# A new opening table, row-wise exponentials for two batches, and block products for one more unit in an attention-and-MLP kernel

## The chip, the cores and the metric

The kernel runs on one core of one Trainium2 chip. The time is device microseconds of that core, median of three runs. The core has five engines that the text names as the profile does: PE (matrix products) with PEld (its weight loads), DVE (vector work), ACT (activations and copies), POOL (vector work without access to the accumulators) and SP, which only issues DMA transfers. Each engine carries out its own list of instructions in order, and waits where an instruction needs another engine's result or a landed transfer.

## The reference

```python
a = softmax(phi, axis=tokens)                 # phi: 8 batches, 8 heads, 576 tokens, 32 memory rows
k_m = einsum('bhsm,bhsd->bhmd', a, k)         # 32 memory rows of 64 per head
v_m = einsum('bhsm,bhsd->bhmd', a, v)
scores = (q @ k_m.T) / sqrt(64)
attn = softmax(scores, axis=memory rows)
x = (attn @ v_m), heads side by side          # 4608 tokens x 512
h = x @ w_in                                  # 512 x 2048, given as 64-bit floats
g = h - tanh(h)
out = g @ w_out                               # 2048 x 512, given as 64-bit floats
```

All 4608 tokens (8 batches of 576) go through both halves. The result is 32-bit.

## The kernel before

**Tiling.** The 4608 tokens are 18 units of 256 (`u` = 0 to 17); the hidden width 2048 is four blocks of 512 (`fb` = 0 to 3). A unit and a block make one slot: `mm1` (L540) computes h for the slot, ACT and DVE turn it into g by a polynomial in three steps (`g1` L555 with its squares L547 and L560 on ACT, `g2` L564, then the 16-bit high part L569 and the low part L574), and `mm2` (L617) or `mm2_blocks` (L666, L673) multiplies g with w_out. Numbers are carried as pairs of 16-bit high and low parts, so that a product of two pairs is three 16-bit products.

**Attention.** For each batch the memory rows of phi, k and v are pooled (`V`, L194 and L202, accumulated in `pkv`), normed (`N`, L207 to L210), turned (`U`, L231), and multiplied with q (`S`, L246); softmax over the memory rows follows (`AM`, `AE`, `AD`, `AT`), and the result is split into high and low (`AS`, L481 and L483). The values are not multiplied with the attention weights but with w_in first: `P` (L492) makes a 256-row matrix per batch and block, high part on ACT (L505), low part on DVE (`PL`, L510) or by PE and ACT (`PLp`, L517 and L519). `mm1` then takes attention weights times that matrix.

**The softmax of phi.** `X` (L144) takes the largest phi of each memory row on DVE and spreads it on a diagonal matrix (L146); a product with ones (`XP`, L155) puts the maxima on every partition; DVE subtracts them (`Y`, L160 and L166) from a second copy of phi that was loaded with the tokens on the partitions (`FA`, L104); ACT takes the exponentials (L180).

**The weights.** `T` converts a pair of weight blocks from 64-bit floats with six integer operations on DVE (L354, L359, L364), and ACT makes the high halves (L376). Low halves come in one of three ways: `Lp` on PE and ACT (four products, L397 and L398, and one copy, L400), `L` on ACT and POOL (L405, L408), `Lv` on DVE (L389). There are 16 such pairs.

**The order.** Up to the second block of unit 4 the order is a table of words, `START`, read from left to right; a word that stands twice or three times is done in as many parts. The words `i0:us`, `o2:gg` and the like issue the load of a weight block into a buffer of that name. `Z` issues products into a result that nobody reads (`warm`, L742). All engines' lists follow from this one table. After it a loop over slots 18 to 71 issues `mm1`, `g1`, `g2`, a slot of `mm2` two slots behind, and tasks from tables by slot: the remaining batches' attention, the block forms of w_out (`G`, L599), and in `PLAN_C` the sums over the weights that test whether all numbers are in the range for which the fast path is exact. That test ends in one number, `bad`; where it is set, a slow path is run.

**Block products.** Units 5 to 17 use `mm2_blocks`: the high-times-high product is done whole (eight products of 512 columns, L666), and the two mixed ones by seven products of half-size blocks (28 products of 256 columns, L673), for which DVE makes four sums of blocks of g per slot (`a_forms`, L587) and eight of w_out once (`b_form`, L599). Units 0 to 4 use `mm2`, 24 products of 512 columns. At a unit's end `evict` (L722 to L734) puts the parts together and stores them.

## Time and profile before

| | before |
|---|---|
| median of three runs | 678.07 us (677.39 to 678.25) |
| the profiled execution | 677.7 us |
| its span (first to last instruction) | 675.9 us |
| PE busy | 640.8 us, 95% |
| DVE busy | 510.7 us, 76% |
| ACT busy | 375.7 us, 56% |
| POOL busy | 256.1 us, 38% |
| mean granted PE clock | 0.993 |

The span leaves 1.8 us of the profiled execution outside it. Busy times are sums over the span without overlaps; a PE product is counted from its start to a modelled end, so PE looks busier than its work. In the views quoted below, a row of the timeline reads: start, duration, engine, line, operation, output and inputs, shapes, count, and in brackets the idle time before it and what ended it. A window reads: its bounds, its length, then the busy time of PE, PEld, DVE, ACT and POOL with the number of instructions, the granted PE clock, the busy share of the DMA engines and GB/s. A row of a group reads: count, busy time and mean nanoseconds of one, idle time before them.

### The profile page before, as it was taken

To read this page: it belongs to the slowest core of one execution; us is meant where nothing else is said; L and a number is where in the kernel's file an instruction comes from. 1 tells how busy PE (TensorE), PEld (TensorE's weight loads), DVE (VectorE), ACT (ScalarE), POOL (GpSimd) and SP (SyncE) were. 2 spreads that over 40 slices of the span, in tenths; PEclk is the share of its full clock that TensorE was granted. 3 is DMA by queue.
4 is the path that set the end of the run, shared out by engine and by line. 5 is a ranking of instruction groups with operands and counts; after the bars stand their busy time and mean duration, and the time that the engine had idled before them with its cause. 6 is when DMAs were issued, how large, how long until landed. Compare 5 with 4: busy or idle time off the path is not lost.

```text
span 675.9 us, 15441 instructions
## 1 busy us (share of the span) xinstructions
PE 640.8 (95%) x6628; PEld 447.2 (66%) x6628; DVE 510.7 (76%) x784; ACT 375.7 (56%) x506; POOL 256.1 (38%) x170
## 2 busy tenths in 40 slices
PE   4678989999999999999999999999999999999996
PEld 1336465565646567786767777777777777887874
DVE  4688999989655577965697868886888586867673
ACT  1558477765533355653565455646554587666541
POOL 0032623423111334452345344534453555455521
PEclk9979999999999999999999999999999999999999
DMA  9679663422313132214331523152415224234201
GB/s 342 265 280 363 244 180 125 172 99 86 119 63 107 60 125 72 66 62 176 102 106 42 192 80 121 49 192 68 134 49 190 72 103 121 72 118 137 77 32 37
DMA packets 26428, 86.16 MB, mean 127 GB/s; under 512 B 2928, under 2 KB 3184, under 8 KB 25584
## 3 DMA queue, kind: packets, MB, share of 16 engines
q1 hardware_dynamic: 25056, 82.87, 35.9%
q10 hardware_dynamic: 1296, 2.23, 0.9%
q8 instruction: 54, 0.88, 0.6%
q14 instruction: 22, 0.18, 0.1%
HBM read 73.55 MB, written 11.53 MB: 126 GB/s over the span
## 4 chain that ended last, share of the span: by engine, by line
PE 69%; DVE 6%; ACT 1%; DMA 1%; issue 0%; SPq 0%; DVEq 0%; ACTq 0%
PE hs L540 19%; PE o L666 12%; PE x L673 12%; PE o L673 9%; PE o L617 7%; PE h L540 2%; PE pp L492 2%; PE pkv L194 2%; DVE f L587 2%; PE o1h L617 2%; DVE h L555 1%; DVE h L564 1%; PE psc L246 1%; DMA kv<-in_kva_dram 1%; ACT u L547 1%
## 5 line engine op out<-in xcount | busy, mean ns | idle before, releaser
L574 POOL TENSOR_TENSOR g<-h,g 128x1024 f16<-128x1024 f32 x64 | 145.2, 2268 | 321.8 <-ACT g L569 212.5
L540 PEld LDWEIGHTS <-ph 128*128 128x128 f16 x2304 | 176.6, 98 | 21.9 <-issue 6.5
L540 PE MATMUL hs<-ah,ph 128*128 128x256 f16 (+3 forms) x1088 | 145.8, 248 | 0.0
L555 DVE SCALAR_TENSOR_TENSOR h<-hs,u 128x1024 f32<-128x1024 f32 x52 | 63.5, 1221 | 96.3 <-ACT u L547 96.3
L569 ACT ACTIVATE g<-h 128x1024 f16<-128x1024 f32 x72 | 76.0, 1055 | 94.8 <-DVE h L564 86.0
L540 PE MATMUL hs<-al,ph 128*128 128x256 f16 (+3 forms) x544 | 122.2, 248 | 0.0
L560 ACT ACTIVATE u<-u,beta 128x1024 f32<-128x1024 f32 x72 | 82.6, 1148 | 61.5 <-DVE h L555 61.0
L666 PE MATMUL o<-wout_hi,g 128*128 128x512 f16 x416 | 100.7, 380 | 1.5 <-DVE r L733 1.5
L564 DVE SCALAR_TENSOR_TENSOR h<-u,h 128x1024 f32<-128x1024 f32 x72 | 89.0, 1236 | 5.0 <-ACT u L560 4.6
L673 PEld LDWEIGHTS <-f 128*128 128x128 f16 x832 | 81.3, 98 | 9.5
L617 PEld LDWEIGHTS <-g 128*128 128x128 f16 x480 | 45.7, 98 | 59.4 <-issue 4.1
L547 ACT ACTIVATE u<-hs 128x1024 f32<-128x1024 f32 x52 | 53.0, 1019 | 53.1 <-PE hs L540 53.1
L617 PE MATMUL o<-wout_hi,g 128*128 128x512 f16 x256 | 78.6, 380 | 1.3 <-DVE g L574 0.8
L673 PE MATMUL x<-bt,f 128*128 128x256 f16 x624 | 76.6, 273 | 0.0
L673 PEld LDWEIGHTS <-g 128*128 128x128 f16 x624 | 60.5, 98 | 21.7 <-issue 0.8
L666 PEld LDWEIGHTS <-g 128*128 128x128 f16 x416 | 38.4, 98 | 48.5 <-issue 13.6
L587 DVE TENSOR_TENSOR f<-g 128x512 f16<-128x512 f16 x104 | 59.7, 614 | 3.9 <-POOL g L574 3.4
L540 PE MATMUL h<-ah,ph 128*128 128x256 f16 (+2 forms) x448 | 55.8, 243 | 0.0
L540 PE MATMUL h<-al,ph 128*128 128x256 f16 (+2 forms) x224 | 48.0, 242 | 1.0 <-DVE al L483 1.0
L617 PE MATMUL o<-wout_lo,g 128*128 128x512 f16 x128 | 48.6, 380 | 0.0
L510 DVE SCALAR_TENSOR_TENSOR ph<-pp,ph 128x1024 f16<-128x1024 f32 x30 | 36.5, 1216 | 1.9 <-ACT ph L505 1.7
L505 ACT ACTIVATE ph<-pp 128x1024 f16<-128x1024 f32 x32 | 32.5, 1016 | 4.0 <-PE pp L492 4.0
(134 smaller groups left out, 945.6 us busy)
## 6 DMA issues: line engine op xcount, KB each, us to landing
kv<-in_kva_dram SPq DMA_DIRECT2D x20, 516.0 KB, 4.0
q<-in_qt_dram SPq DMA_DIRECT2D x16, 576.0 KB, 4.1
chk<-in_w_in_dram SPq DMA_DIRECT2D x16, 512.0 KB, 5.2
chk<-in_w_out_dram SPq DMA_DIRECT2D x16, 512.0 KB, 3.4
out_dram<-r SPq DMA_DIRECT2D x25, 256.0 KB, 2.6
kv<-in_kva_dram SPq DMA_DIRECT2D x6, 1032.0 KB, 10.6
raws<-in_w_in_dram SPq DMA_DIRECT2D x12, 512.0 KB, 6.0
raw<-in_w_out_dram SPq DMA_DIRECT2D x12, 512.0 KB, 6.7
```

The source lines that it names most:

```text
L510: nc.vector.scalar_tensor_tensor(pl, pa, S_P / (S_V * S_W), ph, op0=ALU.mult, op1=ALU.subtract)
L540: nc.tensor.matmul(hp[:, k, tu : tu + w], px[:, g, cs], d[ax][:, g, ta : ta + w], start=(n == 0), stop=(n == 5),)
L547: nc.scalar.activation(uu, hp, AF.Square, scale=1.0 / (S_A * S_P))
L555: nc.vector.scalar_tensor_tensor(h3, hp, C2 * S_G / (S_A * S_P), uu, op0=ALU.mult, op1=ALU.mult)
L560: nc.scalar.activation(uu, uu, AF.Square, bias=c["beta"])
L564: nc.vector.scalar_tensor_tensor(h3, uu, CC, h3, op0=ALU.add, op1=ALU.mult)
L569: nc.scalar.activation(gg[:, 0], h3, AF.Copy)
L574: eng.tensor_tensor(gg[:, 1], h3, gg[:, 0], op=ALU.subtract)
L587: nc.vector.tensor_tensor(o, x, y, op=op)
L617: nc.tensor.matmul(o, gx[:, k, P * tt : P * tt + P], wx[:, 4 * fb + k, :], start=(first and k == 0 and wx is wout_hi and gx is gh), stop=( ...
L666: nc.tensor.matmul(o[th], gg[:, 0, k, P * th : P * th + P], wout_hi[:, 4 * fb + k, :], start=(first and k == 0), stop=False)
L673: nc.tensor.matmul(dst, a(1 - n, kk), b(n, kk), start=(new and kk == 0 and n == 0), stop=(end and kk == 1 and n == 1))
```

## The change

1. **Constants first.** The 16-bit identity and its scaled copies (L1052 to L1054) are made by DVE ahead of all else, so `Z` products may begin at once; in the kernel before, DVE converted the first weight pair ahead of them. A `Z` word is now two products, not four, and there are 26 of them, not 4.
2. **Exponentials in rows.** For batches 0 and 1, `X` takes the negated maxima (L144's operation, no diagonal); `YX` takes the exponentials on ACT straight from the row-wise copy of phi with the maxima as bias, two instructions of 576 columns; `XT` turns them with ten products by the identity on PE, and ACT copies the result out of the accumulators in two pieces. The second copy of phi (`FA0`, `FA1`), the diagonal, the product with ones and the subtraction are gone for these two.
3. **The table.** `START` is a new order throughout. Counted by words: low halves by PE for three pairs, not five; by DVE for four more blocks (two pairs); one `PLp` became `PL`; one low part of g moved from POOL to DVE, one multiplication and one split from DVE to POOL. The block forms `G` of w_out stand in its last third, and the forms of the first block of unit 4 at its end.
4. **Unit 4 by block products.** `mm2_blocks` and `evict` now serve unit 4 too, with the sums of its blocks of g by DVE.
5. **Norms.** For three of the four blocks of w_in, DVE adds the four squared rows together (`SS`, two additions), so that `NI` takes 4 products, not 16.
6. **The end.** In the last unit the second half's products are split by column halves, the first into an accumulator of their own, so that half of its result is put together earlier; the half is stored by one transfer, issued by ACT, not by two. The number `bad` is read before the last `evict`.

On DVE, the first instructions of the program. `wt` are converted weights, `raw` their 64-bit source, `nid`, `nidp`, `idw` the identities, `pt` phi in rows. Before:

```order
L354 TENSOR_SCALAR wt_105<-raw_101 128x512
L354 TENSOR_SCALAR wt_106<-raw_103 128x512
L359 SCALAR_TENSOR_TENSOR wt_105<-raw_101,wt_105 128x512
L359 SCALAR_TENSOR_TENSOR wt_106<-raw_103,wt_106 128x512
L364 SCALAR_TENSOR_TENSOR wt_105<-raw_101,wt_105 128x512
L364 SCALAR_TENSOR_TENSOR wt_106<-raw_103,wt_106 128x512
L1052 TENSOR_SCALAR nid_66<-ident 128x128
L1053 TENSOR_SCALAR nidp<-ident 128x128
L1054 TENSOR_SCALAR idw<-ident 128x128
L354 TENSOR_SCALAR wt_137<-raws_134 128x512
```

Now:

```order
L1093 TENSOR_SCALAR nid_66<-ident 128x128
L1094 TENSOR_SCALAR nidp<-ident 128x128
L1095 TENSOR_SCALAR idw<-ident 128x128
L380 TENSOR_SCALAR wt_108<-raw_101 128x512
L380 TENSOR_SCALAR wt_109<-raw_106 128x512
L385 SCALAR_TENSOR_TENSOR wt_108<-raw_101,wt_108 128x512
L385 SCALAR_TENSOR_TENSOR wt_109<-raw_106,wt_109 128x512
L390 SCALAR_TENSOR_TENSOR wt_108<-raw_101,wt_108 128x512
L390 SCALAR_TENSOR_TENSOR wt_109<-raw_106,wt_109 128x512
L186 TENSOR_REDUCE mx_124<-pt_122 128x2
L380 TENSOR_SCALAR wt_141<-raws_126 128x512
```

The identities went ahead of the first conversion, and the maxima of phi (L186, before L144), which stood behind four conversions, now stand behind one.

On PE, what stands ahead of the first pooling `pkv`. `pw` are low halves of weights (five pairs of them in the whole table before, three now), `pmx` the spread maxima, `pet` and `pel` the turned exponentials. Before, with twelve `warm` products ahead of the first `pw` and four behind it:

```order
L397 MATMUL pw_212<-wt_182,idw 128x512
L398 LDWEIGHTS nid_66
L398 MATMUL pw_212<-win_hi,nid_66 128x512
L397 MATMUL pw_212<-wt_183,idw 128x512
L398 LDWEIGHTS nid_66
L398 MATMUL pw_212<-win_hi,nid_66 128x512
L155 MATMUL pmx_228<-dg_208,ones 128x256
L194 MATMUL pkv_234<-kv_164,e_158 32x129 x16
L194 MATMUL pkv_234<-kv_168,e_158 32x129 x16
L202 MATMUL pkv_234<-kt_166,e_158 32x129 x8
```

Now, with 36 `warm` products ahead of the first `pw`:

```order
L423 MATMUL pw_206<-wt_142,idw 128x512
L424 LDWEIGHTS nid_66
L424 MATMUL pw_206<-win_hi,nid_66 128x512
L200 MATMUL pet_211<-ident,pt_122 128x128 x8
L202 MATMUL pel_212<-ident,pt_122 64x128 x2
L786 LDWEIGHTS nid_66
L786 MATMUL warm<-nid_66 128x512
...
L220 MATMUL pkv_234<-kv_166,e_229 32x129 x16
```

`pw_212` was the fourth pair in this place and `pw_206` is the second: two pairs' low halves left PE's list ahead of the pooling, the product with ones left it, and the ten turning products came in.

On DVE, the end of the program. `r` are the results, `x`, `o` and `oh` accumulators, `bad` the number read. Before:

```order
L722 SCALAR_TENSOR_TENSOR r_8605<-x,r_8605 128x256
L723 SCALAR_TENSOR_TENSOR r_8606<-x,r_8605 128x256
L724 TENSOR_TENSOR r_8605<-r_8605,r_8606 128x256
L725 TENSOR_TENSOR r_8606<-r_8606 128x256
L733 SCALAR_TENSOR_TENSOR r_8605<-o_8449,r_8605 128x512
L730 SCALAR_TENSOR_TENSOR r_8606<-o_8450,r_8606 128x256 x2
L1061 TENSOR_LOAD bad
```

Now:

```order
L925 TENSOR_LOAD bad
L765 SCALAR_TENSOR_TENSOR r_8676<-x,r_8676 128x256
L766 SCALAR_TENSOR_TENSOR r_8677<-x,r_8676 128x256
L767 TENSOR_TENSOR r_8676<-r_8676,r_8677 128x256
L777 SCALAR_TENSOR_TENSOR r_8676<-o_8507,r_8676 128x512
L770 TENSOR_TENSOR r_8677<-r_8677 128x256
L774 SCALAR_TENSOR_TENSOR r_8677<-oh,r_8677 128x256
L774 SCALAR_TENSOR_TENSOR r_8677<-o_8508,r_8677 128x256
```

The load went to the front, the sum L725 behind the first half's eviction, and only one operation of 256 columns still reads an accumulator that the last products write.

```diff
 START = """
-i0:us i1:gg T00 T00 T00 T00 Z00 Z00 Z00 Lp00 Lp00 i6:kv3 T03 T03 T03 i4:kv2 i3:pp2 T02 i2:gg FX0 FA0 T02 T02 KA0 KB0
...
+i0:gg Z00 i1:gg T00 T00 Z00 T00 T00 Z00 FX0 X0 i6:kv3 YX0 Z00 Z00 Z00 Z00 Z00 T03 T03 T03 i2:gg Z00 Z00 Z00 Z00 Z00
...
+    def top_bias(self, b, d):
+        mx = self.big.tile([P, 2], F32, tag="mx", name=f"mx{b}")
+        self.tc.nc.vector.tensor_reduce(mx, d["pt"], axis=AX.X, op=ALU.max, negate=True)
+        d["mx"] = mx
+
+    def expo_rows(self, b, d):
+        for r in range(2):
+            self.tc.nc.scalar.activation(d["pt"][:, r], d["pt"][:, r], AF.Exp, bias=d["mx"][:, r : r + 1])
+
+    def expo_turn(self, b, d, ps, ps_tail):
...
+        for c in range(4):
+            for r in range(2):
+                nc.tensor.matmul(pe[:, 2 * c + r], pt[:, r, P * c : P * c + P], self.c["ident"], start=True, stop=True)
+        for r in range(2):
+            nc.tensor.matmul(pb[64 * r : 64 * r + 64, 0:P], pt[:, r, 512:S], self.c["ident"], start=True, stop=True)
+        yield
+        d["e"] = self.big.tile([P, 9, 128], F32, tag="e", name=f"e{b}", bufs=1)
+        nc.scalar.activation(d["e"][:, 0:8], pe, AF.Copy)
+        nc.scalar.activation(d["e"][:, 8], pb[:, 0:P], AF.Copy)
...
+    def squares_sum(i):
+
+        sq = acc["q", i]
+        nc.vector.tensor_tensor(sq[:, 0:2], sq[:, 0:2], sq[:, 2:4], op=ALU.add)
+        nc.vector.tensor_tensor(sq[:, 0], sq[:, 0], sq[:, 1], op=ALU.add)
...
+        blocks = 1 if fb < 3 else 4
         for k in range(4):
-            for pr in range(4):
+            for pr in range(blocks):
...
         def main(th):
+            if th and u == NUNIT - 1:
+                for dst, cs, end in ((acc["h1"], hi, last), (o[1][:, lo], lo, False)):
+                    for k in range(4):
+                        nc.tensor.matmul(
+                            dst, gg[:, 0, k, P : 2 * P], wout_hi[:, 4 * fb + k, cs],
+                            start=(first and k == 0), stop=(end and k == 3),
+                        )
+                return
...
             if u == NUNIT - 1 and th == 1:
-                for cs, q in ((hi, nc.sync), (lo, nc.scalar)):
-                    nc.vector.scalar_tensor_tensor(r[:, cs], o[th][:, cs], sc, r[:, cs], op0=ALU.mult, op1=ALU.add)
-                    q.dma_start(out[t0 + P :, cs], r[:, cs])
+                for cs, p in ((hi, acc["h1"]), (lo, o[1][:, lo])):
+                    nc.vector.scalar_tensor_tensor(r[:, cs], p, sc, r[:, cs], op0=ALU.mult, op1=ALU.add)
+                nc.scalar.dma_start(out[t0 + P :, :], r)
...
-        for _ in range(4):
+        for _ in range(2):
             nc.tensor.matmul(
...
-        (18, "G00"), (18, "; G01"), (19, "; G10 G11"), (20, "; G20 G21"), (21, "G30 ; G31 CE CQ CQ"), (22, "CW"), (23, "CW"), (24, "CW"), (30, "CE CQ"), (31, "CW CE SI0"), (32, "CW CW | NI0"),
+        (21, "; CE CQ CQ"), (22, "CW"), (23, "CW"), (24, "CW"), (30, "CE CQ"), (31, "CW CE SI0"), (32, "CW CW ; SS0"),
...
-    forms = []
+    forms = [(4, 1)]
     for sl, (u, fb) in enumerate(slots, 18):
-        if sl == 20:
+        if sl == 18:
             acc["x"] = ps_h.tile([P, 2, 512], F32, tag="h", name="x")
             acc["hp"] = ps_h.tile([P, 4, UT], F32, tag="h", name="hs")
...
-        (mm2 if v < 5 else mm2_blocks)(v, vb, vb == 0, vb == NFB - 1)
-        if v == 4 and vb == NFB - 1:
-            go(f"O{v}")
+        mm2_blocks(v, vb, vb == 0, vb == NFB - 1)
...
+    c["wide"] = nc.values_load(c["bad"][0:1, 0:1], min_val=0, max_val=1)
     evict()
-    in_order(tc, first)
+    in_order(tc, c["first"])
```

More of the change, by code (lines that the diff above doesn't have):

```diff
@@ L786, in go @@
                 return
-    first = len(nc.cur_bb.bb.instructions)
     for word in START.split():
@@ L1060, in tile_kernel @@
         split_path(inner, tc, c, ins, out)
[L1061 to L1062 removed]
+    with tc.If(c["wide"] > 0):
         with ExitStack() as inner:
```

59 lines of the change are left out of this document (32 added, 27 removed), and 4 rows, old and new, of the table PLAN_C.

## The prediction

> **What bounds the kernel now.** First the page's busy times, then the windows by stage (the last bound is where the last product starts), to see which engine is full where.
>
> ```profile
> PE 640.8 (95%) x6628; PEld 447.2 (66%) x6628; DVE 510.7 (76%) x784; ACT 375.7 (56%) x506; POOL 256.1 (38%) x170
> 0.00:10.00 10.00, 0.85 (x3) 0.31 (x4) 4.31 (x12) 2.52 (x3) 0.95 (x10) 1.00 0.81 285
> 10.00:20.00 10.00, 10.00 (x28) 4.30 (x27) 6.26 (x13) 2.22 (x4) 0.00 (x0) 1.00 1.03 422
> 20.00:30.00 10.00, 5.44 (x36) 2.49 (x37) 5.90 (x10) 6.14 (x8) 0.00 (x0) 1.00 0.72 291
> 30.00:40.00 10.00, 4.93 (x132) 2.51 (x122) 7.73 (x17) 2.43 (x9) 2.22 (x2) 0.92 0.70 242
> 40.00:52.35 12.35, 11.24 (x116) 5.18 (x109) 10.43 (x21) 7.97 (x12) 3.69 (x4) 0.79 0.72 264
> 52.35:60.00 7.65, 7.27 (x110) 6.33 (x112) 5.78 (x10) 5.94 (x8) 2.28 (x2) 1.00 1.01 401
> 60.00:148.70 88.70, 83.69 (x839) 48.93 (x829) 85.86 (x123) 60.98 (x88) 33.15 (x18) 1.00 0.51 176
> 148.70:209.20 60.50, 60.25 (x538) 34.62 (x537) 42.63 (x50) 28.51 (x30) 12.67 (x7) 1.00 0.28 95
> 209.20:669.80 460.60, 457.16 (x4864) 342.56 (x4861) 341.08 (x532) 258.94 (x348) 201.12 (x128) 1.00 0.30 99
> ```
>
> Three stages. From 148.7 us on PE is full: 60.25 of 60.50 us, then 457.16 of 460.60. From 60 to 148.7 us DVE is (85.86 of 88.70), with PE close behind. Up to 52.35 us, where DVE takes its first `g1`, nobody is: DVE works 34.63 us (the five windows' sum) and idles 17.7. PE's waits and the timeline say on what.
>
> ```profile
> PE pkv L194 <- ACT e L180: 3.4, 2, 3.0
> ...
> 1.12 0.29 POOL masks.py:199 TENSOR_SCALAR_AFFINE_SELECT ident<-ident 128x128 f32<-128x128 f32 x1
> 8.87 0.22 DVE L1052 TENSOR_SCALAR nid<-ident 128x128 f16<-128x128 f32 x1
> 9.15 5.30 PE L742 MATMUL warm<-nid 128*128 128x512 f16 x12 [9.15 <-DVE nid L1052]
> 9.95 1.29 DVE L359 SCALAR_TENSOR_TENSOR wt<-raws,wt 128x512 uint32<-128x512 uint32 x2
> 15.53 0.43 DVE L354 TENSOR_SCALAR wt<-raws 128x512 uint32<-128x512 uint32 x1 [3.10 <-issue]
> 17.42 1.02 PE L397 MATMUL pw<-wt,idw 128*128 128x512 f32 x2
> 22.43 1.35 DVE L144 TENSOR_REDUCE mx<-pt 128x2 f32<-128x1152 f32 x1
> 23.81 0.42 DVE L146 TENSOR_TENSOR dg<-ident,mx 128x256 f32<-128x256 f32 x1
> 28.20 1.16 ACT L180 ACTIVATE e<-e 128x1152 f32<-128x1152 f32 x1 [1.17 <-DVE e L166]
> 29.41 0.86 PE L194 MATMUL pkv<-kv,e 128*32 128x129 f32 x22 [3.02 <-ACT e L180]
> 31.88 0.16 DVE L207 TENSOR_SCALAR kr<-pkv 128x2 f32<-128x2 f32 x1 [3.72 <-PE pkv L202]
> 32.84 0.66 PE L231 MATMUL ptr<-ident,kvn 128*64 128x128 f32 x8 [1.07 <-DVE kvn L210]
> 39.52 0.65 PE L492 MATMUL pp<-win_lo,vh 64*32 64x512 f16 x8
> 47.86 0.41 PE L492 MATMUL pp<-win_lo,vh 64*32 64x512 f16 x8
> 52.35 1.22 DVE L555 SCALAR_TENSOR_TENSOR h<-h,u 128x1024 f32<-128x1024 f32 x1
> ```
>
> One chain runs through this: the identity at 8.87 (behind the first conversion), twelve warming products at 0.43 us each, only then the first low half on PE, whose source buffers the third conversion must overwrite (DVE idles 3.10 us to 15.53); the maxima of phi at 22.43 behind four conversions, the exponential at 28.20, the pooling, the norm at 31.88, softmax, the first `g1` at 52.35. PE's clock is at half for some 0.08 x 10.00 x 2 + 0.21 x 12.35 x 2 = 6.8 us between 30 and 52 us; the same eight products take 0.65 us there and 0.41 later.
>
> **The change part by part.**
>
> *Opening, up to the norm of batch 0.* The identity is ready at 1.4 us (row of 1.12) and DVE waits for its first weights anyway, so products start near 1.9. At 0.43 us for as long as before (5.3 us), then at 0.22 (below: 1.73 us for eight), 36 of them end at 7.2 + 24 x 0.216 = 12.4. The first low half so starts at 12.4 instead of 14.2; it is four products, 2.1 us, of which 1.02 is each 32-bit one. DVE: first conversion to 8.9 as before, maxima to 10.3, second conversion (0.86 and twice 1.29, a little overlapped) to 13.5, third from about 14 to 17.5, fourth to 20.8. The exponentials run on ACT from 10.3. The turning products wait for the second low half (to 17.0). Their price is not in the trace: by L231's row four small 32-bit products take 0.66, so ten take 1.65; by L397's row ten take 10.2; their 128 columns are a quarter of L397's, 2.6, and I take 3. ACT's copy of 128x1024 is about L505's 1.02, the small one less: done at 21.3. Pooling took 29.41 to 31.88; with two pairs of warming products inside (0.86) it ends at 24.6. The norm is 7.3 us earlier. Bounds: 8.6 with the cheap turns, nothing with the dear ones.
>
> ```profile
> L505 ACT ACTIVATE ph<-pp 128x1024 f16<-128x1024 f32 x32 | 32.5, 1016 | 4.0 <-PE pp L492 4.0
> L389 DVE SCALAR_TENSOR_TENSOR wout_lo<-wt,wout_hi 128x512 f16<-128x512 f32 x10 | 6.4, 678 | 0.6 <-ACT wout_hi L376 0.5
> L510 DVE SCALAR_TENSOR_TENSOR ph<-pp,ph 128x1024 f16<-128x1024 f32 x30 | 36.5, 1216 | 1.9 <-ACT ph L505 1.7
> L160 DVE TENSOR_TENSOR e<-e,pmx 128x1024 f32<-128x1024 f32 x4 | 4.9, 1217 | 4.0 <-PE pmx L155 4.0
> L166 DVE TENSOR_TENSOR e<-e,pmx 64x128 f32<-64x128 f32 x8 | 2.3, 281 | 0.1
> ```
>
> *From the norm to the first `g1`.* 52.35 - 31.88 = 20.5 us before. If the warming products keep the clock up, half of what ran at half speed comes back, at most 3.4 us; some lies beside other waits, and new DVE work stands in the chain, so I take 1: first `g1` near 44, 8.3 us earlier. DVE's list ahead of it lacks two diagonals (0.84), one subtraction (1.22 + 0.56) and four instructions of a later conversion (0.86 + 1.29); it has two low halves (1.36) and one low part of P (1.22) more: 2.2 us less work. So DVE has idled 44 - (34.6 - 2.2) = 11.6 instead of 17.7: 6.1 us less.
>
> *The DVE stretch.* Over all of the table DVE loses two diagonals and two subtractions (4.4), a split and a multiplication (about 1.5), and gains four low halves (2.7), one low part of P (1.2), one of g (1.2): 0.8 us less; the block forms come on top, at its end. A list as long that has idled 6.1 us less ends 6 to 7 us earlier, if it stays as full: **6.5**. PE has the room: its list loses work (two pairs of low halves, one `PLp`) where it was waiting, and in the PE stretch nothing is moved onto it.
>
> ```profile
> L599 DVE TENSOR_TENSOR bt<-wout_hi 128x2048 f16<-128x2048 f16 x2 | 2.4, 1222 | 0.0
> L587 DVE TENSOR_TENSOR f<-g 128x512 f16<-128x512 f16 x104 | 59.7, 614 | 3.9 <-POOL g L574 3.4
> 217.59 5.18 PE o L617 x24
> 633.07 1.73 PE o L666 x8
> 635.67 1.75 PE x L673 x16
> 663.79 0.76 DVE L587 TENSOR_TENSOR f<-g 128x512 f16<-128x512 f16 x2 [3.39 <-POOL g L574]
> 333.97 0.54 PE L429 MATMUL pni<-ones,sqi 128*128 128x1 f16 x16
> PE o L666 <- DVE r L733: 1.5, 4, 1.0
> 669.81 0.76 DVE L730 SCALAR_TENSOR_TENSOR r<-o,r 128x256 f32<-128x256 f32 x2 [0.20 <-PE o L673]
> ```
>
> *Block forms and unit 4.* Eight forms of 1.22 (9.8 us) and the sums of one block (2.1 to 2.5) now lie ahead of 209 us on DVE, which idles 60.50 - 42.63 = 17.9 there: hidden; without that cover, 12 us. A slot of unit 4 on PE was 5.18; now 1.73 + 28 x 1.75/16 = 4.79, four times 0.39: **1.6**. The other three blocks' sums on DVE take the place of the forms that left. Unit 4's `evict` may cost what the row of 1.5 us for four shows, 0.4; I leave it to the range.
>
> *Norms.* 16 products 0.54, four a quarter: 3 x 0.40 = **1.2** on a full PE. The two additions (some 1 us by L599's and L587's rows) fall into slots where DVE idles over a quarter of the time (341.08 of 460.60 us busy).
>
> *End.* Two operations of 0.76 follow the last product now, one then: **0.35**. One store takes the place of two; the load of `bad` leaves a place where it held nobody.
>
> Sum for the profiled execution: 677.7 - 6.5 - 1.6 - 1.2 - 0.35 = 668.05. The median stands 0.37 above that execution: **668.4 us**.
>
> The rows say of the clock: half speed for the 5.3 us after the first product, and half again near 40 us though PE's longest wait by then was 3.0. The Trainium skill ("TensorE: Matmul & The Clock Gate", Part 1, "What's actually happening") has the clock rise after one busy window of about 3.4 us and fall only after an idle one as long. By it the 36 products would end at about 11.4, an estimate from that page, and the sum be 667.5; the trace agrees with neither figure.
>
> **The rivals.**
>
> *The early start does not carry.* The norm comes early but the new order makes DVE wait elsewhere: for the turned exponentials of batch 1, for buffers whose loads stand in SP's one list behind others, or because the turns cost 10. For it: 60 to 148.7 us idles only 2.8 us, the mark of an order fitted closely, and any new one has its own misfits. Against: the wait on `e` and the subtraction are gone. Half the opening is lost: 671.5 to 675.
>
> *The warming products block PE.* 36 of them stand ahead of the first low half. If the clock stays at half through all, they end at 1.9 + 36 x 0.43 = 17.4, and everything behind runs at half: low halves 4.2 each, turns 6, pooling 5: the norm near 38, 6 us later than before, of which the other terms give back 3.2: 680.5, slower. It decides the sign once the products' pace is still 0.43 at about 12 us. Against: the same products at the same spacing got full speed after 5.3 us.
>
> *DVE's two-input work is blocked by POOL.* L587's first pair has a mean of 614 ns, though behind POOL's end (row of 663.79) two take 0.76. If forms and sums cost the 1.2 of L599 apiece, unit 4 and the norms need 16 x 0.6 + 6 x 0.7 = 14 us more on DVE; a third in PE's way costs 4.6: 673. The Trainium skill ("SBUF — State Buffer", section "SBUF: two separate sides") has such an operation wait for the whole POOL instruction. By that rule this rival would be likely; the trace agrees that the times spread, but DVE's idle share has paid for it so far.
>
> *More than forecast.* DVE's idle after the first `g1` (1.87 + 2.84 us) goes too, with the wait on the spread maxima of batch 1: 663.5.
>
> **How the numbers follow.** Forecast 0.62 (its own range 665 to 671.5), early start lost 0.16, blocked PE 0.07, blocked DVE 0.07, more 0.08. The range 663 to 675.5 leaves out the blocked PE and the edges. A difference of 0.2%, 1.4 us, is about what a measurement here can tell from none. Faster: 0.90 (forecast, more, and nearly all of two rivals); same 0.02; slower 0.08.
>
> **What would show it.** Warming products from 2 us, their pace 0.43 turning to 0.22 near 7; L207's successor near 24.6; first `g1` near 44; PE clock 1.00 from 30 to 50 us; DVE's first 16 conversions done 6 to 7 us earlier; slots of unit 4 at 4.8 us on PE; the last DVE operation 0.4 after the last product. It is wrong if the norm comes after 29, if the DVE stretch idles over 6 us, or if PE waits over 3 us in all between slot 18 and the end.

## The result, and the profile after

The changed kernel took 665.34 us (median of four runs, 665.18 to 666.03) against 678.06 of the kernel before (677.39 to 678.25): a ratio of 0.982, interval 0.981 to 0.983. That is 12.7 us less where 9.7 were forecast. The profiled execution took 665.18 us, its span 663.3.

The windows by stage of the changed kernel, cut at the same places of the program as those of before (the first `g1`; the twelfth; that of slot 18, the nineteenth; the start of the last products). Columns as in the prediction:

```profile
0.00:44.20 44.20, 37.89 (x333) 18.70 (x334) 35.75 (x63) 22.54 (x36) 11.40 (x17) 0.96 0.95 365
44.20:140.10 95.90, 90.92 (x933) 55.23 (x933) 94.83 (x138) 66.80 (x97) 33.67 (x20) 1.00 0.51 184
140.10:199.80 59.70, 59.70 (x536) 34.31 (x535) 51.15 (x60) 28.62 (x30) 14.45 (x7) 1.00 0.26 85
199.80:657.40 457.60, 453.90 (x4889) 347.98 (x4888) 346.08 (x547) 258.05 (x348) 199.34 (x128) 1.00 0.30 99
```

Up to the first `g1` DVE idled 8.45 us (44.20 - 35.75); before it was 17.7. From there to 140.1 it idles 1.07 of 95.90 us, where before it was 4.71 of 96.35 (1.87 and 2.84 in the two windows). Together 9.5 instead of 22.4: 12.9 us less idle, while DVE had 4.3 us more to do (130.6 against 126.3: four more low halves of w_in, two of them slowed, and the sixteenth conversion, less the subtractions; the eight block forms all stand behind 140.1, from 146.0 to 193.1). The difference, 8.6 us, is how much earlier this stretch ends.

The timeline of the opening: start, duration, engine, line, operation, output and inputs, shapes, count, and the idle time before it with its cause.

```profile
1.70 10.33 PE L786 MATMUL warm<-nid 128*128 128x512 f16 x36 [1.70 <-DVE nid L1093]
11.86 1.02 PE L423 MATMUL pw<-wt,idw 128*128 128x512 f32 x2
14.57 0.43 DVE L380 TENSOR_SCALAR wt<-raws 128x512 uint32<-128x512 uint32 x1 [0.84 <-DMA raws<-in_w_in_dram]
16.59 1.95 PE L200 MATMUL pet<-ident,pt 128*128 128x128 f32 x16
18.46 0.44 PE L202 MATMUL pel<-ident,pt 128*64 128x128 f32 x4
18.68 4.40 POOL L434 TENSOR_TENSOR win_lo<-wt,win_hi 128x512 f16<-128x512 f32 x2 [17.12 <-ACT wt L431]
19.02 1.00 ACT L205 ACTIVATE e<-pet 128x1024 f32<-128x1024 f32 x1
20.08 1.09 PE L220 MATMUL pkv<-kv,e 128*32 128x129 f32 x32 [0.64 <-ACT e L205]
20.75 2.88 DVE L415 SCALAR_TENSOR_TENSOR win_lo<-wt,win_hi 128x512 f16<-128x512 f32 x2 [0.24 <-ACT win_hi L402]
23.55 0.15 DVE L233 TENSOR_SCALAR kr<-pkv 128x2 f32<-128x2 f32 x1
44.22 1.21 DVE L588 SCALAR_TENSOR_TENSOR h<-h,u 128x1024 f32<-128x1024 f32 x1
```

The norm of batch 0 comes at 23.55 instead of 31.88, the first `g1` at 44.22 instead of 52.35. The ten turns took 2.3 us (counted as 20 in the rows, two for each 32-bit product). The norm does not wait for the pooling, whose last products end at 23.1: DVE takes it right behind two low halves (L415) that take 2.88 us together beside POOL's L434, where two alone take some 1.4 (678 ns each by the row of L389). Nor do the first products with q (`S`) wait for the norm. Their keys are ready at 25.5, and PE waits until 26.26 for the load of q, which stands in SP's list behind a load of weights and is issued at 20.92:

```profile
PE psc L272 <- DMA q<-in_qt_dram: 1.1, 1, 1.1
```

In the kernel before, that load was issued at 14.15, and `S` waited for the keys.

How the time went along the program: the start of `g1` in the changed kernel less that in the kernel before, in the two profiled executions.

```
g1 number     1     12    19 (slot 18)   24 (unit 4 done)   31     52     72    span
shift, us   -8.1   -8.7      -9.4             -11.0        -12.4  -12.2  -11.8  -12.6
```

So 9.4 us come by slot 18, 1.6 in unit 4, 1.4 in one step near number 31, 0.6 are lost behind it, and the end gives 0.8. The step of 1.4 is a transfer: in the kernel before PE waited there 1.2 us for the second half of k and v. The waits of PE from 205 us on, before:

```profile
PE pkv L194 <- DMA kv<-in_kva_dram: 1.2, 1, 1.2
```

and after:

```profile
PE o L707 <- DVE r L777: 2.7, 4, 1.0
PE pkv L220 <- DMA kv<-in_kva_dram: 0.4, 1, 0.4
```

The wait for the load shrank; that for `evict`, which was 1.5 us over four, grew to 2.7.

The end of the changed kernel, and the transfers by issuer (KB each, median us from issue to landing):

```profile
657.39 0.60 PE L714 MATMUL o<-bt,g 128*128 128x256 f16 x4
657.60 0.41 DVE L770 TENSOR_TENSOR r<-r 128x256 f32<-128x256 f32 x1
658.46 0.41 DVE L774 SCALAR_TENSOR_TENSOR r<-o,r 128x256 f32<-128x256 f32 x1
out_dram<-r ACTq DMA_DIRECT2D x1, 256.0 KB, 2.4
```

The transfer that ended the kernel before:

```profile
out_dram<-r ACTq DMA_DIRECT2D x1, 128.0 KB, 3.0
```

DVE still ends 0.9 us behind the last product, as before (0.8): the sum L770 stands behind the first half's `evict` and pushes the half that was to be early. What is earlier lies behind the issue of the last store: from there to the end of the span it took 4.4 us, before 5.3. The one larger store landed 0.6 us sooner than the smaller one did. But in both kernels some 2 us pass between that landing and the end, in which SP goes through its last waits. These begin 3.0 us (before 3.4) behind SP's branch around the slow path, and SP, which has one store less to issue in the last half, comes to that branch 0.8 us ahead of the last store's issue and not just behind it. So the landing is one candidate and SP's list the other; by the rows SP's list ends later.

### The profile page after: what moved, and what is told of

It reads as the page before. It is cut to its first block, busy times and chain, and to the rows that moved or that the text cites. A ratio compares the mean times of both kernels' runs of the same rounds, so it can differ in the third digit from the quotient of the medians.

```text
span 663.3 us, 15588 instructions
## 1 busy us (share of the span) xinstructions
PE 643.0 (97%) x6690; PEld 456.5 (69%) x6690; DVE 529.2 (80%) x808; ACT 376.0 (57%) x509; POOL 258.9 (39%) x171
## 4 chain that ended last, share of the span: by engine, by line
PE 74%; DVE 19%; ACT 3%; issue 2%; DMA 2%; POOL 0%; SPq 0%; DVEq 0%; ACTq 0%; POOLq 0%
PE hs L573 17%; PE x L714 12%; PE o L707 11%; PE o L714 8%; PE o L650 8%; PE h L573 5%; DVE f L620 3%; PE pp L525 3%; DVE h L597 3%; DVE h L588 2%; PE pkv L220 2%; PE warm L786 2%; PE o1h L650 2%; DVE wt L390 1%; ACT u L580 1%
## 5 line engine op out<-in xcount | busy, mean ns | idle before, releaser
L607 POOL TENSOR_TENSOR g<-h,g 128x1024 f16<-128x1024 f32 x63 | 138.4, 2197 | 311.4 <-ACT g L602 213.7
L573 PE MATMUL hs<-ah,ph 128*128 128x256 f16 (+3 forms) x1152 | 151.5, 246 | 0.0
L573 PE MATMUL hs<-al,ph 128*128 128x256 f16 (+3 forms) x576 | 127.6, 246 | 0.0
L707 PE MATMUL o<-wout_hi,g 128*128 128x512 f16 x432 | 104.7, 380 | 2.7 <-DVE r L777 2.7
L714 PEld LDWEIGHTS <-f 128*128 128x128 f16 x896 | 87.7, 98 | 10.1
L714 PE MATMUL x<-bt,f 128*128 128x256 f16 x672 | 82.5, 273 | 0.0
L620 DVE TENSOR_TENSOR f<-g 128x512 f16<-128x512 f16 x112 | 63.4, 606 | 3.9 <-POOL g L607 3.4
L650 PE MATMUL o<-wout_hi,g 128*128 128x512 f16 x192 | 58.6, 379 | 0.7 <-DVE g L607 0.7
L573 PE MATMUL h<-ah,ph 128*128 128x256 f16 (+3 forms) x384 | 49.9, 246 | 0.6 <-DVE ph L543 0.6
L573 PE MATMUL h<-al,ph 128*128 128x256 f16 (+2 forms) x192 | 42.4, 246 | 0.0
L650 PE MATMUL o<-wout_lo,g 128*128 128x512 f16 x96 | 36.4, 379 | 0.0
```

What stands on the lines that cost most here:

```text
L573: nc.tensor.matmul(hp[:, k, tu : tu + w], px[:, g, cs], d[ax][:, g, ta : ta + w], start=(n == 0), stop=(n == 5),)
L607: eng.tensor_tensor(gg[:, 1], h3, gg[:, 0], op=ALU.subtract)
L620: nc.vector.tensor_tensor(o, x, y, op=op)
L650: nc.tensor.matmul(o, gx[:, k, P * tt : P * tt + P], wx[:, 4 * fb + k, :], start=(first and k == 0 and wx is wout_hi and gx is gh), stop=( ...
L707: nc.tensor.matmul(o[th], gg[:, 0, k, P * th : P * th + P], wout_hi[:, 4 * fb + k, :], start=(first and k == 0), stop=False)
L714: nc.tensor.matmul(dst, a(1 - n, kk), b(n, kk), start=(new and kk == 0 and n == 0), stop=(end and kk == 1 and n == 1))
```

## The experiments

Each kernel is the changed one with one edit, unless it says otherwise; all times are medians, and the kernel before took 677.3 to 677.7 beside each of them. First the changed kernel once more.

**The changed kernel again.**

> The changed kernel itself again, beside the three that are compared with it here. Its first measurement was 665.34 us. In its profile the second halves of the k and v loads of the late batches landed in 4.5 us; in the profile with the old norms they took 5.2 to 5.9 and the products waited for them, 1.3 us at one slot and 0.7 at another. If such landings are chance of an execution, this second profile of the same kernel shows its own pattern of slow and quick landings, with steps of 0.5 to 1.3 us in the start of g1 at the slots that follow a slow one, and the start of the first g1 differs by up to 1 us. If the landings are set by the order, every landing is again within 0.3 us of the first profile.

It took 665.33 us (665.15 to 666.29). Its profiled execution, one of 666.29, has its first `g1` 0.4 us later than the first profile and a step of 0.4 near number 55, no other above 0.2 from slot 18 on. The landings of the second halves of k and v were within 0.35 us of the first profile in the late batches (4.46 to 5.46 us from issue). One earlier load, issued near 206 us, took 6.55 us where it had taken 4.96. So the landings of the late batches repeat in these two executions, which differ by 1 us, in the opening and in that one step.

**The exponentials as before**, at the same places of the table.

```diff
-N_ROWS = 2
+N_ROWS = 0
-... FX0 X0 i6:kv3 YX0 ... XT0 T02 o3:pp5 L02 XT0 ...   FX1 ... X1 YX1 ... XT1 ... XT1 ...
+... FX0 X0 i6:kv3 FA0 ... XP0 Y0 T02 o3:pp5 L02 Y0 ...  FX1 ... X1 FA1 ... XP1 Y1 ... Y1 ...
```

> The changed kernel with the old exponentials for batches 0 and 1 (second copy of phi loaded, maxima spread by a product, subtraction on DVE) at the places in the table where the new ones stood. Theory of the early start (the norm of batch 0 sets when DVE fills up): the norm comes later by the second copy's 1.4 us of loading and the subtraction's 1.8 us, some 3 us, and the end by 3 to 6 us as DVE also has 4.4 us of work more: 669 to 671. Rival (warming products and constants first made the early start): within 2 us of 665.3.

It took 670.84 us (670.21 to 675.01): the rows are worth 5.5. The timeline of its opening, from the execution that took 675.01:

```profile
19.47 1.21 DVE L162 TENSOR_TENSOR e<-e,pmx 128x1024 f32<-128x1024 f32 x1
22.45 1.95 PE L220 MATMUL pkv<-kv,e 128*32 128x129 f32 x32 [5.81 <-ACT e L182]
27.96 0.16 DVE L233 TENSOR_SCALAR kr<-pkv 128x2 f32<-128x2 f32 x1 [1.88 <-PE pkv L228]
```

The subtraction stands on DVE behind two conversions; PE idles 5.81 us for it, the pooling then runs at half pace (1.95 for what takes 1.09 in the changed kernel), and the norm comes at 27.96, 4.4 us later. In this execution, the longest of its kernel, the clock was at half for 20.5 us of the first 73, so its shape is a hint and the median the measure.

**Constants behind the first conversion.**

```diff
+    first = len(nc.cur_bb.bb.instructions)
-    in_order(tc, c["first"])
+    in_order(tc, first)
```

> The changed kernel with its constants made behind the first conversion of weights, as in the kernel before (all else as changed, the 36 products ahead of the first low half too). The products can then start only near 9 us instead of 1.7. Theory of the prediction (identity first is a part of the gain, since the products wait for it): 36 products from 9.2, 5 us of them at half pace and the rest at 0.22, end near 19.5 instead of 11.9, the norm of batch 0 comes 5 to 7 us later (29 to 31 instead of 23.6), the whole 670 to 673. Rival: the norm is set by the landing of the weights and by ACT's exponentials; then it moves by less than 2 us and the whole stays below 668.

It took 671.9 us (671.38 to 672.25), 6.6 more, as the theory of the prediction has it. Its timeline:

```profile
8.95 9.87 PE L786 MATMUL warm<-nid 128*128 128x512 f16 x36 [8.95 <-DVE nid L1094]
18.65 1.02 PE L423 MATMUL pw<-wt,idw 128*128 128x512 f32 x2
19.77 0.43 DVE L380 TENSOR_SCALAR wt<-raws 128x512 uint32<-128x512 uint32 x1 [6.28 <-PE pw L423]
```

The first low half starts 6.8 us later, and DVE waits 6.28 us for the buffers that it empties. From there the shift of `g1` stays at 5.6 to 6.9 us to the end.

**Constants first in the kernel before**, its table and its products untouched.

```diff
-    in_order(tc, first)
+    in_order(tc, c["first"])
```

> The kernel before with one edit: the 16-bit identity and its copies are made ahead of the first conversion, as in the changed kernel; its table and its four Z words of four products stay. Theory of the prediction (the identity at 8.87 and the twelve products behind it hold up the first low half and so the norm): products from 1.7, the first low half near 9.6 instead of 14.45, the third conversion no longer waits 3.1 us for its buffers, the norm 3 to 5 us earlier, the whole 673 to 675. Theory after the other runs (leaving the warming products out of the changed kernel did not move its norm, 23.34 against 23.24, though its first low half started 3.4 us earlier; DVE's list and ACT's, fed by weight loads, set it): DVE's list behind the third conversion gains at most the 3.1 us, the norm 1 to 3 us earlier, the whole 675.5 to 677. If the whole stays within 1 us of the kernel before, constants first is worth nothing without the new table.

It took 674.75 us (673.28 to 675.05) against 677.5: 2.75 less, ratio 0.995 (0.994 to 0.997). From its timeline, the norm:

```profile
28.36 0.16 DVE L207 TENSOR_SCALAR kr<-pkv 128x2 f32<-128x2 f32 x1 [4.63 <-PE pkv L202]
```

The norm is 3.5 us earlier (28.36 against 31.88), the first `g1` 3.1; from the third to number 54 the shift is 3.0 to 3.3, behind that 2.5. This is within what the prediction's theory wanted (3 to 5 us, 673 to 675), near its smaller end; DVE's wait of 3.1 us for the buffers of the third conversion is gone, and that is about its size.

**No warming products at all** (the 26 words `Z` left out).

> The changed kernel without any of its warming products (all 26 words Z left out; no result changes). Theory: the products hold the PE clock up, so that without them the pooling, the turns and the products from the norm to the first g1 run at half speed; granted PE clock at half for over 20 of the first 44 us, the low halves 4 us a pair, the turns over 4, the first g1 at 46 to 49 instead of 44.2, the whole 667 to 670. Rival: the landing of the weights (third conversion at 14.57 us in the changed kernel) and DVE set the pace of the opening; then the first g1 stays within 1 us of 44.2 and the whole within 1 us of the changed kernel, or is quicker by up to 1, since the first low half starts when its weights are ready near 10 us and not at 11.9.

It took 667.02 us (666.62 to 667.48), 1.7 more. Its timeline:

```profile
8.25 2.07 PE L423 MATMUL pw<-wt,idw 128*128 128x512 f32 x2 [8.25 <-DVE wt L390]
16.91 0.44 PE L202 MATMUL pel<-ident,pt 128*64 128x128 f32 x4
18.82 1.00 ACT L205 ACTIVATE e<-pet 128x1024 f32<-128x1024 f32 x1
23.34 0.15 DVE L233 TENSOR_SCALAR kr<-pkv 128x2 f32<-128x2 f32 x1
```

The first low half starts 3.6 us earlier, at half pace, the turns are done 1.5 us earlier, and yet the copy of the exponentials and the norm stand where they stood (18.82 and 23.34, against 18.71 and 23.24 in the changed kernel run beside it). ACT takes the copy behind the high halves and L431, and these wait for the conversion whose source lands at 14.4 us (14.57 in the first profile). Behind the copy ACT makes two more high halves, and DVE's low halves (L415) wait for these; the norm follows them without idle time in both runs. So the products neither help nor hurt up to the norm. What they give lies behind it: without them the clock was at half for 10.24 us from 25.95 on, with them for 3.41, and the first `g1` came 1.5 us later than in the run beside it.

**Twice the warming products.**

```diff
-        for _ in range(2):
+        for _ in range(4):
```

> The changed kernel with four products to each Z word, not two: 72 ahead of the first low half, and four instead of two inside the opening. It tries the rival that the warming products block PE, by doubling them. By their measured pace (5 us at 0.43, then 0.22) 72 end at 1.7 + 5 + 60 x 0.216 = 19.7 instead of 11.9. If PE's list sets the norm from there on, it comes 7 to 8 us later (31), the whole 672 to 674. If the norm has slack against PE (it did not move when the products were left out), it moves by 7.8 less the slack, which the wait of the exponential's copy shows as at most 1.5 to 2.5 us: norm 28.5 to 30, the whole 670 to 672. If the clock gets more even, the half-speed stretch near 27 us goes and 0.8 comes back.

It took 674.13 us (672.43 to 674.43), 8.8 more. Its timeline:

```profile
1.70 18.56 PE L786 MATMUL warm<-nid 128*128 128x512 f16 x72 [1.70 <-DVE nid L1093]
32.05 0.16 DVE L233 TENSOR_SCALAR kr<-pkv 128x2 f32<-128x2 f32 x1 [0.72 <-PE pkv L228]
```

The first low half starts at 20.09, 8.2 later, the norm is 8.5 later than in the first profile and the first `g1` 7.4. The clock was at full from 7.5 us to the end of the work, and that did not pay for it. In its profile 7.6 us are there by slot 18; waits for k and v loads near numbers 31 and 47 add most of the rest. With the run before it: work taken off PE ahead of the norm gains nothing, work put there costs nearly all of itself, since 36 products let PE's turns end just as ACT comes to copy them (18.46 + 0.44 and 19.02).

**Unit 4 by whole products, as before** (`mm2`; no sums of its blocks of g).

```diff
-        mm2_blocks(v, vb, vb == 0, vb == NFB - 1)
+        (mm2 if v < 5 else mm2_blocks)(v, vb, vb == 0, vb == NFB - 1)
```

> The changed kernel with unit 4 by whole products (24 of 512 columns a slot) and its own store, the forms of w_out still in the opening. Theory of the sum: four slots of 0.39 us, 666.9; g1 of slots 18 and earlier unmoved, of slot 23 and later 1.6 us later. Rival (DVE's sums for unit 4 and its evict cost PE as much as the products save): within 0.4 us of 665.3.

It took 667.74 us (667.41 to 668.4), 2.4 more. Against the first profile of the changed kernel `g1` shifts by +0.8 at number 19 and +1.2, 1.6, 2.0, 2.4 at 20 to 23: 0.4 for each of the four slots, 1.6 in all, and nothing at the unit's end. The profiled execution is one of 668.4, 3.2 above the first profile; the rest of that is 0.8 from the opening and 0.7 from a wait for a k and v load near number 31.

**The norms as before** (16 products a block, no additions), twice.

```diff
-        blocks = 1 if fb < 3 else 4
+        blocks = 4
-        ... (31, "CW CE SI0"), (32, "CW CW ; SS0") ... (33, "NI0") ...
+        ... (31, "CW CE SI0"), (32, "CW CW | NI0") ...
```

> The changed kernel with the norms as before: 16 products per block of w_in at the end of slots 32, 40 and 48, no additions on DVE. Theory of the sum (the norms' products lie on a full PE): 3 x 0.4 us slower than the changed kernel's 665.3, so 666.5. Rival (what PE saves there, 0.3 us each, it then waits for DVE at the unit's end, because the two additions push a reciprocal's chain behind POOL and the next g1 with it): 665.0 to 665.4, and from slot 31 to slot 53 the starts of g1 stand within 0.3 us of the changed kernel's.

> The changed kernel with the norms as before (16 products a block, no additions), a second time. Its first measurement was 668.19 us, 2.9 more than the changed kernel, though in its profile the 16 products cost only 0.3 us a block more and PE's wait for evict fell from 2.7 to 1.5 us; the rest was products that waited for k and v loads, 2.2 us over four. Theory A (those landings are chance of an execution or of a chip): the median comes to 665.3 to 666.3, and the waits for these loads fall under 1 us. Theory B (the order without the additions makes these loads land late): the median is again 667.5 to 668.8, and the profile shows again three or four waits for these loads, near slots 39 and 47.

It took 668.19 us (667.68 to 668.81), and again 668.31 (666.18 to 669.90): 2.9 and 3.0 more. The waits of PE and the timeline around slot 32, where the additions of the changed kernel stand, first without them:

```profile
PE pkv L220 <- DMA kv<-in_kva_dram: 2.2, 4, 0.9
PE o L707 <- DVE r L777: 1.5, 4, 1.0
322.18 0.18 DVE L313 TENSOR_SCALAR sz<-sz 128x18 f32<-128x18 f32 x1
325.27 1.23 DVE L588 SCALAR_TENSOR_TENSOR h<-hs,u 128x1024 f32<-128x1024 f32 x1 [2.61 <-ACT u L580]
```

and in the changed kernel:

```profile
322.03 0.68 DVE L453 TENSOR_TENSOR sqi<-sqi 128x1024 f16<-128x1024 f16 x1
322.75 0.42 DVE L454 TENSOR_TENSOR sqi<-sqi 128x512 f16<-128x512 f16 x1
323.34 2.13 POOL L607 TENSOR_TENSOR g<-h,g 128x1024 f16<-128x1024 f32 x1 [4.19 <-issue]
323.87 1.63 DVE L313 TENSOR_SCALAR sz<-sz 128x18 f32<-128x18 f32 x1
324.18 0.24 PE L462 MATMUL pni<-ones,sqi 128*128 128x1 f16 x4
325.72 1.16 DVE L588 SCALAR_TENSOR_TENSOR h<-hs,u 128x1024 f32<-128x1024 f32 x1
```

The two additions, 1.1 us, fall into idle time as forecast, but they push an operation of the softmax behind the start of POOL's: 0.18 us become 1.63, it ends as POOL does, the next `g1` has no idle time left ahead of it, and `evict` behind it comes later (2.7 instead of 1.5 us). In the profiles that takes back the 0.3 us a block that the products save. What makes the old norms slower by 2.9 is not this. In both profiles `g1` number 72 comes 1.4 us later than in the first profile of the changed kernel, but the span ends 2.6 and 2.8 later: 1.2 and 1.4 us come behind the last store, where no norm stands. SP waits there for the end of PE's list, 2.1 us in the second profile, 0.6 in the changed kernel, and in the first:

```profile
SPq L1140 <- PEq L1140: 1.9, 2, 1.4
```

The rest is waits for k and v loads, 2.2 us over four in the first profile and 1.1 over two in the second, the longest at different slots (behind numbers 38 and 46), with landings up to 5.95 us where the changed kernel's took 4.5 to 5.5. Two medians at the same place speak against chance; the second profile has not the three or four waits that the other theory wanted. Why PE's list ends later in that order, and why these loads land later, stays open.

**The end as before.** Products, `evict` and stores of the last half, and the place of the load of `bad`, as in the kernel before.

> The changed kernel with the old end: whole products for the last half, two operations of 256 columns after them, two stores of 128 KB on two queues, the number read last. Theory of the sum (one DVE operation less after the last product): 0.35 us slower, 665.7. Rival (DVE ends 0.9 us after the last product in both; what ended earlier is the store, 2.4 us from issue to landing against 3.0): 0.7 to 0.8 us slower, 666.1, with the last DVE operation as far behind the last product as in the changed kernel and the last transfer landing 3.0 us after its issue.

It took 665.91 us (665.46 to 669.12), 0.6 more, its `g1` number 72 0.2 earlier and its span 0.7 longer. Its DVE ends at 658.6, no later than in the changed kernel (658.9); its last store is slower, and SP's last waits begin later behind its branch (3.0 in the changed kernel):

```profile
out_dram<-r ACTq DMA_DIRECT2D x1, 128.0 KB, 3.1
SPq L1091 <- SPq L1091: 3.4, 1, 3.4
```

So the end's gain is not DVE's. It lies behind the last store's issue, 5.4 us to the end of the span against 4.4; whether the store's landing or SP's list makes it, no run separates. The difference of the medians is small beside the spread of this run's times.

**Two tries at something better.** Both let POOL do the sum L770 in the last unit, and move the additions out of the way of the softmax. In the first they and their products come one slot later; in the second the additions come at the end of their slot and the products stay.

```diff
-        ... (32, "CW CW ; SS0") ... (33, "NI0") ...
+        ... (32, "CW CW") ... (33, "; SS0") ... (34, "NI0") ...
```

```diff
-        ... (32, "CW CW ; SS0") ... (33, "NI0") ...
+        ... (32, "CW CW | SS0") ... (33, "NI0") ...
```

> The changed kernel with two edits: the two additions of the squared rows and their 4 products one slot later each (a slot in which DVE has no part of a softmax), and in the last unit the sum of the second half's parts by POOL instead of DVE. In the changed kernel the additions pushed a 0.18 us operation of the softmax behind POOL, where it took 1.63, and PE's wait for evict grew from 1.5 to 2.7 us over four; DVE did four operations in a row after the first half's last product and ended 0.9 us after the last product. Theory: the wait for evict goes back to 1.5 (1.2 us less), and the end loses 0.35: 663.5 to 664.5 against 665.3 of the changed kernel. Rival: the wait for evict comes from the slots themselves, or the late additions block the next forms instead: then only the end's 0.35 is seen, 665.0, or nothing.

> The changed kernel with the two additions of the squared rows at the end of their slot, behind the softmax sums of the other batch, with the 4 products left in the next slot; and in the last unit one sum by POOL instead of DVE. The earlier attempt with the products one slot later cost 22.9 us, since they then stood behind P's products and waited three times for an accumulator that DVE empties late (17.9 us of PE's waits). Theory: the 0.18 us operation of the softmax is no longer behind POOL, PE's wait for evict falls from 2.7 to about 1.5 us over four, the end gains 0.35: 664 to 664.8 against 665.3. Rival: the additions themselves now fall behind POOL and delay the next g1 as much as before: 665.0 (the end alone), or later, if the products wait for them.

They took 688.21 us (687.53 to 691.34) and 673.83 (670.95 to 674.8), 22.9 and 8.5 more. PE's longest wait in each, first and second:

```profile
PE pni L462 <- DVE ph L543: 17.9, 3, 6.1
```

```profile
PE pni L462 <- DVE sqi L454: 5.8, 3, 2.0
325.95 2.22 DVE L454 TENSOR_TENSOR sqi<-sqi 128x512 f16<-128x512 f16 x1
325.42 2.47 POOL L607 TENSOR_TENSOR g<-h,g 128x1024 f16<-128x1024 f32 x1 [4.20 <-issue]
```

One slot later the four small products stand behind `P`'s on PE and need an accumulator that DVE empties only after the next `g1`: 6 us, three times, each followed by 6.8 us at half clock. In the second try, at the end of the slot, the second addition falls behind POOL (2.22 us instead of 0.42), and the four products, next on PE, wait 2 us for it; 2.1 us of this profile's loss come in the opening, where it has no edit. Where the additions stand now they cost the least of the three places. From `g1` number 72 to the end of the span these two are 0.1 to 0.2 us shorter than the changed kernel: that is what POOL's sum is worth, of the 0.35 expected, though DVE ends 0.5 after the last product and not 0.9. No version beat the changed kernel.

## Why the prediction was right, and where its sizes were off

**Forecast and sum.** Faster, by the mechanism that it named first: the opening, then a DVE stretch that ends earlier, then a full PE that passes the gain on. The likeliest range was 665 to 671.5, and 665.34 lies at its edge. By the profiles: opening and DVE stretch 9.4 (forecast 6.5), unit 4 1.6 (1.6), a k and v load that was late before 1.4 (not forecast), from there to the last slot -0.6 (norms, 1.2), end 0.8 (0.35): 12.6. The 1.4 are no sure gain: in two runs whose program behind slot 18 is that of the changed kernel, without warming products and with twice as many, the same load was late again and took back 0.8 and 1.4 us.

**Opening.** The marks stood: products from 1.70, 36 of them done near 11.9 (12.4 forecast), turns 2.3 us (3 taken of 1.65 to 10.2), first `g1` at 44.2 (44). The norm was 1 us earlier still (23.55 against 24.6). But the step "the first low half so starts at 12.4", from which the norm was worked out by way of PE, is not what sets it: without the products the low half started at 8.25 and the norm did not move. The chain that ends last runs over the landing at 14.57, the conversion, ACT's high halves and the copy at 19.02, and from there not over the pooling but over ACT's next high halves and DVE's low halves at 20.75. The two chains happened to end within half a microsecond of each other: that the norm came near its forecast is in part luck. The step from the norm to the first `g1` had a gate that the sum left out, the load of q, 0.8 us behind the keys. The runs show that the rows and the early constants are needed (5.5 and 6.6 us without them), but as conditions of one start, not as shares: together they exceed the 8.1 us of the first `g1`. The 6.6 are the price of issuing 36 products late; no run makes the constants late without them. What the new table gives by itself no run shows.

**The DVE stretch** is the term that was mis-sized. "A list as long that has idled 6.1 us less" was right in time up to the first `g1`, wrong in content: DVE had done 35.75 us by then, not 32.4, and had idled 9.3 less. Behind it the new order lost its idle too, 1.07 for 4.71, which the prediction gave a chance of 0.08 as "more than forecast". The wait that it named is gone: 4.0 us of DVE over two batches for the spread maxima (the row of L160).

**Unit 4** was right to a tenth, and its `evict` cost nothing at the unit's end. Its cover held: DVE had 8.6 us idle between 140.1 and 199.8.

**Norms.** The products took 0.24 us a block where 16 took 0.54, a saving of 0.3 and not 0.4. The sentence that the additions "fall into slots where DVE idles" was right by the share and wrong by the place: what they displace runs into POOL, and in the profiles that takes the saving back. What the term is worth as a whole, 0 by the profiles' steps or 2.9 by the median without it, hangs on the loads and on the end of PE's list, and is open.

**End.** "Two operations of 0.76 follow the last product now, one then" failed: the sum that was moved behind the first half's `evict` fills the same time. The gain came behind the last store's issue.

**Rivals.** "The warming products block PE": its mechanism is real, each microsecond of products beyond the 36 came through almost whole (8.2 us later, 8.8 slower), but its condition was not met, the pace being 0.22 from 6.56 us on. "DVE's two-input work is blocked by POOL": the blocking is real, and was in the kernel before too. Sums of two inputs (L620) take 0.42 us alone and up to 1.63 beside POOL; the mean of L620's first pair is 606 ns, before 614; one of the eight forms took 2.02 instead of 1.22; the low halves at 20.75 took 2.88 instead of some 1.4. But its price, 4.6 us on PE, was not there: where the forms stand PE is full all the same (59.70 of 59.70 us). The operation that was caught near slot 32 has one input. The Trainium skill ("SBUF — State Buffer", section "SBUF: two separate sides") has a vector operation in a two-port mode, or with two inputs in this memory beside a POOL operation that reads it, wait for the whole POOL instruction that started first; the rows of 323.34 and 323.87 agree: both end at 325.5. That the operation of 323.87 runs in such a mode no run shows. "The early start does not carry" fell: it carried and grew.

**The marks that failed or told nothing.** PE waited 3.7 us from 199.8 to 657.4, above the 3 that were to show an error; 2.7 of it is `evict`. But the kernel before waits 3.4 there too (460.60 - 457.16), so this mark could tell nothing. The sixteenth conversion ended 22.7 us earlier (136.7 against 159.5), mostly because the new order has it ahead of the twelfth `g1` and the old one behind the thirteenth, so it measured the order and not the stretch.

## What to carry to other kernels

Where two chains end within a microsecond, shortening one shows nothing and lengthening it shows everything: find the slack of each by taking work off it, not only by adding. A small operation is not free on an idle engine if what it displaces crosses the start of another engine's long one; and in an in-order engine a small product is placed by the accumulator that it needs, not by its length. Of an early start, ask also what idle time behind it had the same cause, and which wait ends last on the way: here a load of q took the place of the norm.

## What the runs showed of the hardware

The clock falls without a long wait. The windows of the changed kernel around its half-speed stretch (bounds, length, PE busy first, granted clock third from the end):

```profile
23.63:27.04 3.41, 1.46 (x26) 0.77 (x26) 3.27 (x9) 1.14 (x6) 0.00 (x0) 1.00 0.99 376
27.04:30.45 3.41, 3.41 (x22) 0.65 (x20) 2.58 (x6) 1.24 (x3) 1.16 (x1) 0.50 0.98 398
```

of the run without warming products:

```profile
22.54:25.95 3.41, 0.83 (x24) 0.45 (x8) 3.34 (x9) 1.14 (x6) 0.33 (x1) 1.00 1.02 384
25.95:29.36 3.41, 2.86 (x40) 0.64 (x40) 3.08 (x7) 1.23 (x2) 0.12 (x1) 0.50 1.00 405
```

and two that mark the border, one of the kernel before, followed by full speed, and one of the second try, followed by half speed:

```profile
24.81:28.22 3.41, 1.58 (x6) 0.58 (x4) 1.70 (x3) 1.22 (x3) 0.00 (x0) 1.00 0.69 276
41.86:45.27 3.41, 1.80 (x14) 1.31 (x12) 3.41 (x5) 2.27 (x4) 0.00 (x0) 1.00 0.99 365
```

Every change of the clock in the opening comes at a whole number of 3.41 us from the one before. A window with PE busy for 1.46 of 3.41 us was followed by half speed, though the longest single wait in it was 1.1 us. Over all profiles, cut on each one's own raster, no window with PE busy for under 46% of it kept full speed and none with over 53% lost it; between, both happened (1.58 kept it, 1.80 lost it), so the busy share goes far to decide but is not all. From half speed none under 84% rose; the 2.86 above stayed, and so did one of 2.93 in the second try; full windows rose. The Trainium skill ("TensorE: Matmul & The Clock Gate", Part 1, "What's actually happening") has such a free-running window of 3413 ns, which agrees; that it takes an idle one to fall does not fit, unless 43% counts as idle.

The first rise came 2.9 to 6.0 us after the first product in these runs. Eight profiles have this opening: in the four whose clock did not fall ahead of the first `g1`, that comes 0.2 to 0.8 us earlier than in the first profile, in the other three it comes 0.3 to 0.6 later.
